# A sliding-window transformer kernel on one core: second norm and its loads moved ahead of the MLP weights, first three queries transposed by TensorE, work order found anew

## The chip, the cores and the metric

The kernel runs on one core of a Trainium2 chip. A core has five engines that run side by side, each through its own list of instructions in order: TensorE (PE, matrix products; PEld is its loading of weights), VectorE (DVE), ScalarE (ACT), GpSimd (POOL) and SyncE (SP), which here only issues DMAs. They wait for each other through semaphores. The metric is the device time of one execution in microseconds (us). Before the change the median of three runs is 863.51 us (863.23 to 866.3).

## The reference

Two layers, each of them attention followed by an MLP, on 2048 tokens of 576 numbers. Both layers use the same weights. Cut to what matters:

```python
D, H, Dh, W, F = 576, 32, 18, 256, 4608
def A(x):                                   # attention in a window of 256 keys
    q, k, v = split_heads(x @ wqkv)         # 32 heads of 18
    p = softmax(where(0 <= i - j < W, q @ k.T * Dh**-0.5, -1e9))
    return merge_heads(p @ v) @ wo
def B(x):                                   # MLP
    return gelu(layernorm(x) @ w1 + b1) @ w2 + b2
for _ in range(2):
    x = x + A(layernorm(x))
    x = x + B(layernorm(x))
```

`B` normalises its input, and it gets an input that is already normalised; the kernel makes both norms in one, by a changed scale.

## The kernel before, in words

The 2048 tokens are 16 tiles of 128. Four tiles make a chunk, so two layers make eight chunks, 0 to 7. For every chunk the kernel does these stages:

- `ln1_in` (layer 0) or `ln1` (layer 1): the norm. DVE takes statistics (`ln_stats`, L687 and L691), POOL makes 1/sqrt of the variance (`ln_rstd`, L700 and L702), DVE writes the normalised tile `xn` (L718), and `ln_norm_T` turns it (features onto partitions) into `xnTa`. For chunk 0 TensorE turns it (L735, copied from PSUM by ACT, L738), for all others a DMA transpose does (L741).
- `qkv`: projections to queries, keys and values. Chunk 0 uses whole-array matmuls (L797), chunk 1 matmuls that are packed by column groups or run over the whole array (`quad`, L781 and L778), later chunks row pairs (L837). DVE and ACT bring the results from PSUM into `qn` (L861, L858) or `vA` (L849, L847). Queries and keys are then turned into `qT` and `kT` by a DMA transpose on SP (L880), except the keys of chunk 0, which TensorE turns (L874) and ACT copies (L878). Chunk 1 keeps queries in a free half of `x_res` (`qx`) and two keys in `xnTm` (`kx`).
- `E0`/`E`: scores (L909), exponential on ACT (L919), the window mask on POOL (L940), product with the values (L957), division on DVE.
- `tail`: output projection (L1048), residual (L1025), second norm, turned into `xnTm[:, k % 2]` (resource `xm0_` or `xm1_`).
- `G_part`, `mm2`: the MLP in three thirds, first product L1093, GELU L1103, second product L778 or L781. Its weights come in slices from DRAM throughout (`w1_load`, `w2_load`).

Attention of one chunk and MLP of the chunk before it are issued in one mixed order. That order isn't written by hand. Every step is recorded with `add`, with a planned cost, a latency and a priority; `Plan.schedule` then places the steps one by one on the engine where one can start earliest by these costs, and breaks ties by priority. `PL.nudge` is a table of some 500 numbers that shift the priorities of named groups of steps, so it sets the order on all five engines. Until 140 us of its plan the planner also puts matmuls of zeros (`warm`, L674) where it foresees a wait of TensorE above 0.4 us.

The instructions of one engine run strictly in the order planned. A step whose input is late therefore holds up everything behind it on that engine, and that holds for SP's DMAs as well.

The start of the kernel, up to the first MLP matmul, is what the change touches by hand. There the loads stand on SP in this order: tiles 0 to 3 of x, the three weights of the projections, the first slice of `w1`, and only then tiles 4 to 7 of x, whose load names `xa3` (the last turned tile of chunk 0) as a resource it must follow:

```python
xin_load(4, 4, ["xa3"], -6)
...
xin_load(8, 4, ["k3"], -4)
...
ln1_in(1, -0.9)
```

Of the kernel before, what the change touches and what calls it, by code (L numbers as in the profile page):

```python
# [435 lines left out]
def build_kernel(nc, A_x, A_wqkv, A_wo, B_x, B_w1, B_b1, B_w2, B_b2, out):  # L436
    D = 576
# [13 lines left out]
    HB = 288  # L451
# [27 lines left out]
    PL.nudge = {"": -86.31, "b": 23.63, "ea0.0": -264.23, "ea0.1": 170.66, "ea0.2": 170.75, "ea0.p0": -91.12, "ea0.p1": 0.1, "ea0.p2":  # L479
# [150 lines left out]
    def xin_load(a, cnt, reads=(), prio=-10):  # L630
        dma("sp", x_in[:, a:a + cnt, :], x_dram[a * P:(a + cnt) * P, :].rearrange("(t p) d -> p t d", p=P), reads=reads,
            writes=[f"xin{t}" for t in range(a, a + cnt)], cls="x", ring=4,
            cost=0.6, prio=prio)
# [701 lines left out]
```

## Time and profile before

| what | us |
|---|---|
| median of three runs | 863.51 (863.23 to 866.3) |
| the profiled execution | 864.07 |
| its span, first to last instruction | 862.3 |
| TensorE busy in the span | 846.4 (98%) |
| ScalarE busy | 601.2 (70%) |
| VectorE busy | 395.7 (46%) |
| GpSimd busy | 378.6 (44%) |

The profile is one execution. Its page gives busy time by engine, the chain of work that ended last, and the costliest groups of instructions. Other views answer for a stretch of time: a timeline with one row for consecutive instructions of one line (start, duration, and in brackets the idle time before it with what ended it), a list of who waited for whom, and a table of stretches with the busy time of each engine and the granted TensorE clock. The span is 1.77 us shorter than the time of the same execution; that part lies outside what the trace shows.

### The profile page before, as it was taken

Reading aid. Unit: us, or ns where it says so; the run is one execution under the profiler, and the core shown is the slowest. Engines: PE = TensorE matmul, PEld = TensorE weight load, DVE = VectorE, ACT = ScalarE, POOL = GpSimd, SP = SyncE. Lnnn points to the kernel's source line nnn. Section 1 sums busy time; section 2 is a strip of 40 time slices with the busy share of each in tenths; the row PEclk is TensorE's granted clock in tenths of the full one; section 3 lists DMA queues with packets and bytes.
Section 4 is the critical chain, followed back from the end, with each engine's and each line's share of the span. In section 5 each row is a group of like instructions: output and inputs, shape, how many; then the busy total and the mean of one; then the engine's idle time right before and its main releaser. Section 6 shows DMA issues by size and latency. Waiting matters only on the chain.

```text
span 862.3 us, 27890 instructions
## 1 busy us (share of the span) xinstructions
PE 846.4 (98%) x12002; PEld 520.0 (60%) x12002; DVE 395.7 (46%) x949; ACT 601.2 (70%) x757; POOL 378.6 (44%) x563
## 2 busy tenths in 40 slices
PE   8899999999999999999999999999999999999998
PEld 6455556556565565666665655656556555556556
DVE  5787334644356442673426723465223633153012
ACT  5798797688757797476774878738777589853730
POOL 3787454375234662254522655416444276331100
PEclk9999999999999999999999999999999999999999
DMA  9798534743577524985359353594434963446320
GB/s 235 143 187 142 140 96 136 165 126 66 167 161 150 140 72 138 176 142 170 102 124 192 85 164 124 99 204 108 154 122 104 250 190 105 135 133 179 120 84 29
DMA packets 181995, 119.84 MB, mean 139 GB/s; under 512 B 107504, under 2 KB 181872, under 8 KB 181872
## 3 DMA queue, kind: packets, MB, share of 16 engines
q1 hardware_dynamic: 181872, 118.05, 55.6%
q8 instruction: 95, 1.56, 0.8%
q14 instruction: 28, 0.23, 0.1%
HBM read 90.10 MB, written 2.36 MB: 107 GB/s over the span
## 4 chain that ended last, share of the span: by engine, by line
PE 88%; DMA 4%; DVE 2%; POOL 2%; ACT 2%; issue 1%; SPq 0%; POOLq 0%; ACTq 0%
PE ps L1093 30%; PE ps L778 25%; PE ps L781 10%; PE ps L837 8%; PE ps L909 6%; PE ps L957 4%; PE ps L1048 3%; DMA xnTm<-xn 2%; ACT pT L919 1%; DMA xnTa<-xn 1%; PE ps L797 1%; POOL pT L940 1%; DVE xn L718 1%; DVE x_res L1025 1%; DMA qT<-qn 1%
## 5 line engine op out<-in xcount | busy, mean ns | idle before, releaser
L940 POOL TENSOR_SCALAR_AFFINE_SELECT pT<-pT 128x512 bf16<-128x512 bf16 (+1 forms) x368 | 284.3, 794 | 234.7 <-ACT pT L919 228.9
L919 ACT ACTIVATE pT<-ps 128x1024 bf16<-128x1024 f32 (+1 forms) x384 | 345.5, 972 | 49.9 <-PE ps L909 49.2
L1093 PE MATMUL ps<-xnTm,w_sb 64*128 64x512 bf16 x2592 | 290.9, 376 | 1.1 <-DVE vA L849 0.7
L1103 ACT ACTIVATE hT<-ps,b1col 128x512 bf16<-128x512 f32 x276 | 168.1, 688 | 175.3 <-PE ps L1093 175.0
L1093 PEld LDWEIGHTS ps<-xnTm,w_sb 64*128 64x128 bf16 x2592 | 129.6, 94 | 140.4 <-issue 4.8
L778 PE MATMUL ps<-w_sb,hT 128*128 128x288 bf16 x1446 | 193.7, 287 | 1.5 <-DVE x_res L1025 0.7
L1025 DVE TENSOR_TENSOR x_res<-ps,x_res 128x288 f32<-128x288 f32 x224 | 100.3, 453 | 183.5 <-PE ps L778 128.9
L778 PEld LDWEIGHTS ps<-w_sb,hT 128*128 128x128 bf16 x1446 | 133.6, 98 | 52.6 <-issue 17.1
L837 PE MATMUL ps<-wqkv,xnTa 64*128 64x288 bf16 x1296 | 90.8, 283 | 1.8 <-DMA xnTa<-xn 0.6
L781 PE MATMUL ps<-w_sb,hT 128*32 128x288 bf16 x2664 | 91.6, 286 | 0.2
L861 DVE CAST qn<-ps 128x288 bf16<-128x288 f32 x112 | 45.7, 448 | 99.1 <-PE ps L837 88.9
L837 PEld LDWEIGHTS ps<-wqkv,xnTa 64*128 64x128 bf16 x1296 | 61.6, 94 | 28.8 <-issue 3.1
L781 PEld LDWEIGHTS ps<-w_sb,hT 128*32 128x32 bf16 x2664 | 68.4, 97 | 14.9 <-issue 4.6
L968 DVE STREAM_TRANSPOSE oq<-ps 128x512 f32<-128x512 f32 x64 | 45.7, 714 | 66.6 <-PE ps L957 65.5
L909 PE MATMUL ps<-qT,kT 32*128 32x384 bf16 (+2 forms) x1216 | 64.2, 277 | 2.8 <-ACT pT L919 1.6
L700 POOL TENSOR_SCALAR vtmp<-mv_all 128x1 f32<-128x1 f32 (+1 forms) x43 | 8.9, 207 | 111.8 <-DVE mv_all L691 108.3
L687 DVE BATCH_NORM_STATS2 st_all<-x_res 128x6 f32<-128x288 f32 (+1 forms) x128 | 53.5, 445 | 9.0 <-DMA x_res<-in_A_x_dram 8.2
L1109 POOL TENSOR_TENSOR x_res<-x_res,b2bc 128x576 f32<-128x576 f32 x32 | 40.2, 1277 | 39.1 <-ACT hT L1103 38.9
L849 DVE CAST vA<-ps 128x288 bf16<-128x288 f32 x60 | 25.0, 447 | 56.6 <-PE ps L837 55.6
L957 PE MATMUL ps<-pT,vA 128*20 128x384 bf16 (+2 forms) x1408 | 50.4, 275 | 0.0
L909 PEld LDWEIGHTS ps<-qT,kT 32*128 32x128 bf16 x1216 | 19.4, 92 | 42.7 <-issue 29.8
L718 DVE TENSOR_SCALAR xn<-x_res,mv_all,rstd 128x576 bf16<-128x576 f32 (+1 forms) x60 | 34.4, 578 | 21.1 <-DMA xnTm<-xn 9.0
(58 smaller groups left out, 486.8 us busy)
## 6 DMA issues: line engine op xcount, KB each, us to landing
w_sb<-in_B_w_dram SPq DMA_DIRECT2D x46, 864.0 KB, 6.1
w_sb<-in_B_w_dram SPq DMA_DIRECT2D x48, 768.0 KB, 4.8
w_sb<-in_B_w_dram SPq DMA_DIRECT2D x96, 48.0 KB, 4.5
wqkv<-in_A_wqkv_dram SPq DMA_DIRECT2D x3, 576.0 KB, 4.8
x_res<-in_A_x_dram SPq DMA_DIRECT2D x3, 576.0 KB, 4.9
wqkv<-in_B_w_dram SPq DMA_DIRECT2D x2, 864.0 KB, 6.7
out_dram<-x_res SPq DMA_DIRECT2D x12, 144.0 KB, 1.8
wo_sb<-in_A_wo_dram SPq DMA_DIRECT2D x4, 144.0 KB, 3.0
```

The costliest lines, as they stand in the source:

```text
L687: add("dve", lambda e, i=i, s=s: e.bn_stats(st_all[:, t, i, :], s[:, t, i * HB:(i + 1) * HB]), reads=res, writes=[f"st{t}_{i}"], cost=0.37 ...
L778: return e.matmul(bank(b)[:, 0:HB], lhs, rhs, start=start, stop=stop, skip_group_check=True)
L781: ins = e.matmul(bank(b)[32 * j:32 * j + 32, 0:HB], lhs[:, 32 * j:32 * j + 32], rhs, start=start, stop=stop, tile_position=(0, 32 * j), sk ...
L837: ins = e.matmul(bank(bs[o])[:, 0:HB], xnTa[r:r + 64, c, i * 128:(i + 1) * 128], wqkv[r:r + 64, c, col:col + HB], start=(c == 4), stop=(ph ...
L861: add("dve", lambda e, b=bs[o], dst=dst: e.tensor_copy(dst, heads_of(bank(b))), reads=[bs[o]], writes=[f"qn{sl}h{o}"], cost=0.375, lat=0.1 ...
L909: ins = e.matmul(two(bs[j // 2])[:, j % 2, col:col + nq * 128], k_of(T0 + so)[0][32 * j:32 * j + 32, g, :], qs[32 * j:32 * j + 32, g, qo * ...
L919: add("act", lambda e, h2=h2: e.activation(pT[:, sl, 2 * h2:2 * h2 + 2, lo:hi], two(bs[h2])[:, :, lo:hi], ACT.Exp, scale=SCALE), reads=[bs ...
L940: add("pool", lambda e, ap=ap, pat=pat, sgn=sgn, kind=kind: e.affine_select(ap, ap, pattern=pat, compare_op=(ALU.is_ge if kind == "d" else ...
L957: ins = e.matmul(bank(bo)[32 * j:32 * j + VW, qo * 128:(qo + nq) * 128], vA[:, (T0 + so) % VS, 8 * j + g, :], pT[:, sl, j, col:col + nq * ...
L1025: add("dve", lambda e: e.tensor_tensor(x_res[:, t, sl], bank(b)[:, 0:HB], x_old[:, t, sl], ALU.add), reads=[b] + ([f"xin{t}"] if first els ...
L1093: ins = e.matmul(bank(bks[i])[:, 0:n], w1_sb[r:r + 64, sls[i], col:col + 128], xnTm[r:r + 64, k % 2, c, 0:n], start=(c == 4), stop=(ph == ...
L1103: add("act", lambda e, ff=ff, hd=hd, bk=bk: e.activation(hd[:, 0:n], bank(bk)[:, 0:n], ACT.Gelu_apprx_tanh, bias=b1col[:, ff:ff + 1]), rea ...
```

## The change

Seven edits, all in the planner's numbers or at the start of the kernel:

1. The load of tiles 4 to 7 of x no longer follows the turned tiles of chunk 0. It stands right behind the projection weights (priority -9.9).
2. The load of tiles 8 to 11 follows the last turned tile of chunk 1 instead of the last key of chunk 0.
3. Chunk 1's first norm writes into `xnTm[:, 0]` (`xm0_`), not into `xnTa`, so it needn't wait until chunk 0's projections have read `xnTa`. Its 1/sqrt is made for two tiles at a time, not four.
4. The first two slices of `w1` name `k3` (the last turned key of chunk 0) and `xm0_3` (the last turned norm tile of chunk 1) as what they follow. Before, one named `qx0`, which no step had written when the load was recorded, so it was free to go at once; the other named `v0h0`.
5. Queries 0, 1 and 2 of chunk 0 are turned by TensorE and copied by ACT, as the keys were already. Query 3 stays with a DMA transpose.
6. Planned costs of some loads and of the first zero matmuls differ, and a wait of the last partial transpose is stated more fully.
7. The nudge table is another one throughout, so the order differs on every engine from start to end.

```diff
-    PL.nudge = {"": -86.31, "b": 23.63, "ea0.0": -264.23, "ea0.1": 170.66, "ea0.2": 170.75, "ea0.p0": -91.12, "ea0.p1": 0.1, "ea0.p2":
...
+    PL.nudge = {"": -10.17, "b": -4.2, "ea0.0": 160.82, "ea0.1": 46.36, "ea0.2": -22.78, "ea0.p0": -231.95, "ea0.p1": 71.25, "ea1.0":
...
-            cost=0.6, prio=prio)
+            cost=0.45 if a < 4 else 0.6, lat=1.4 if a < 4 else 2.0, prio=prio)
...
-            writes=[f"w{w}A"], cost=0.6, prio=-10)
+            writes=[f"w{w}A"], cost=0.5, lat=1.9, prio=-10)
...
-        add("pe", lambda e, b=b: zero(e, b), reads=["warm"], writes=[b], cost=0.25, lat=0.2, prio=-7, alloc=[b])
+        add("pe", lambda e, b=b: zero(e, b), reads=["warm"], writes=[b], cost=0.42, lat=0.2, prio=-7, alloc=[b])
...
-                add("pe", fn, reads=rd[cs[0] // 4:][:1] + ["ident"], writes=[b], cost=0.1 * len(cs), prio=prio, alloc=[b] if cs[0] == 0 else ())
+                add("pe", fn, reads=rd[:1 + cs[0] // 4] + ["ident"], writes=[b], cost=0.1 * len(cs), prio=prio, alloc=[b] if cs[0] == 0 else ())
...
-            wr = [f"w{w}A", f"xa{i}"] + [f"w{w}{x}{b}" for x in "BC" for b in range(2)]
+            xT, xn_ = (xnTm[:, 0], "xm0_") if k == 1 else (xnTa, "xa")
+            wr = [f"w{w}A", f"{xn_}{i}"] + [f"w{w}{x}{b}" for x in "BC" for b in range(2)]
...
-                if k == 0 and (w == "k"):
+                if k == 0 and (w == "k" or w == "q" and i in (0, 1, 2)):
...
-    xin_load(4, 4, ["xa3"], -6)
+    xin_load(4, 4, ["wvA"] if False else [], -9.9)
...
-    xin_load(8, 4, ["k3"], -4)
...
-        ln_rstd(list(range(t0, t0 + nt)), False, prio)
+            if t % 2:
+                ln_rstd([t - 1, t], False, prio)
...
-            ln_norm_T(t0 + i, i, xnTa, "xa", prio, x_in, [f"xin{t0 + i}"], dup=True)
+            ln_norm_T(t0 + i, i, *((xnTm[:, 0], "xm0_") if k == 1 else (xnTa, "xa")), prio, x_in, [f"xin{t0 + i}"], dup=True)
...
+    xin_load(8, 4, ["xm0_3"], -0.8)
...
-                w1_load(-1, ["v0h0"])
+                w1_load(-0.7, ["xm0_3"])
...
-                w1_load(-1, ["qx0"])
+                w1_load(-1, ["k3"])
```

What stands on SP behind the projection weights, before the change. `w_sb` is a slice of MLP weights, `x_res` from `in_A_x_dram` a load of x, `hT` and `b2bc` the biases, `qT<-qn` a turned query tile, `xnTa<-xn` a turned norm tile:

```order
L626 DMA w_sb<-in_B_w_dram 128x4x768
L626 DMA w_sb<-in_B_w_dram 64x384 x2
L880 DMA_TRANSPOSE qT<-qn 128x8x128 x2
L626 DMA x_res<-in_A_x_dram 128x4x576
L880 DMA_TRANSPOSE qT<-qn 128x8x128
L626 DMA x_res<-in_A_x_dram 128x4x576
L626 DMA hT<-in_B_b_dram 36x128
L626 DMA b2bc<-in_B_b_dram 128x576
L880 DMA_TRANSPOSE qT<-qn 128x8x128
L626 DMA w_sb<-in_B_w_dram 128x4x768
L626 DMA w_sb<-in_B_w_dram 64x384 x2
L741 DMA_TRANSPOSE xnTa<-xn 128x5x128 x4
```

And after it:

```order
L625 DMA x_res<-in_A_x_dram 128x4x576
L740 DMA_TRANSPOSE xnTm<-xn 128x5x128 x3
L880 DMA_TRANSPOSE qT<-qn 128x8x128
L740 DMA_TRANSPOSE xnTm<-xn 128x5x128
L625 DMA x_res<-in_A_x_dram 128x4x576
L625 DMA hT<-in_B_b_dram 36x128
L625 DMA b2bc<-in_B_b_dram 128x576
L625 DMA w_sb<-in_B_w_dram 128x4x768
L625 DMA w_sb<-in_B_w_dram 64x384 x2
```

The load of x and the four norm transposes have moved ahead of both slices of `w1`, and three query transposes are gone from SP. Line numbers after the change are one lower in most of the file.

TensorE in the same stretch, from the first projections to the first score, before:

```order
L797 MATMUL ps<-wqkv,xnTa 128x288 x20
L735 MATMUL ps<-ident,xn 128x128 x10
L797 MATMUL ps<-wqkv,xnTa 128x288 x20
L874 MATMUL ps<-ident,qn 128x128 x8
L797 MATMUL ps<-wqkv,xnTa 128x288 x10
L874 MATMUL ps<-ident,qn 128x128 x8
L797 MATMUL ps<-wqkv,xnTa 128x288 x5
L874 MATMUL ps<-ident,qn 128x128 x8
L797 MATMUL ps<-wqkv,xnTa 128x288 x5
L909 MATMUL ps<-qT,kT 128x384 x4
```

And after, where the last row is again the first score:

```order
L734 MATMUL ps<-ident,xn 128x128 x6
L874 MATMUL ps<-ident,qn 128x128 x8
L796 MATMUL ps<-wqkv,xnTa 128x288 x10
L874 MATMUL ps<-ident,qn 128x128 x8
L796 MATMUL ps<-wqkv,xnTa 128x288 x5
L874 MATMUL ps<-ident,qn 128x128 x8
L796 MATMUL ps<-wqkv,xnTa 128x288 x15
L874 MATMUL ps<-ident,qn 128x128 x8
L734 MATMUL ps<-ident,xn 128x128 x4
L874 MATMUL ps<-ident,qn 128x128 x8
L734 MATMUL ps<-ident,xn 128x128
L909 MATMUL ps<-qT,kT 128x384 x4
```

Five groups of eight query and key transposes stand ahead of the first score instead of three, and 50 of the 120 projection matmuls of chunk 0 instead of 70; two more such groups follow later instead of one.

DVE, before, from the second fetched query or key on. `BN_STATS` and `BN_AGGR` are the statistics, here those of chunk 1, and `CAST` is a result fetched from PSUM:

```order
L861 CAST qn<-ps 128x2x8x18
L718 TENSOR_SCALAR xn<-x_res,mv_all,rstd 128x576
L861 CAST qn<-ps 128x2x8x18 x4
L687 BN_STATS st_all<-x_res 128x6 x3
L691 BN_AGGR mv_all<-st_all 128x2
L687 BN_STATS st_all<-x_res 128x6 x2
L691 BN_AGGR mv_all<-st_all 128x2
```

And after:

```order
L717 TENSOR_SCALAR xn<-x_res,mv_all,rstd 128x576
L861 CAST qn<-ps 128x2x8x18
L686 BN_STATS st_all<-x_res 128x6 x3
L690 BN_AGGR mv_all<-st_all 128x2
L686 BN_STATS st_all<-x_res 128x6
L861 CAST qn<-ps 128x2x8x18
L690 BN_AGGR mv_all<-st_all 128x2
L686 BN_STATS st_all<-x_res 128x6 x3
L861 CAST qn<-ps 128x2x8x18
```

The first statistics of chunk 1 stood behind six fetched query and key results; now they stand behind three, and the fourth and fifth are fetched between them.

More of the change, by code (lines that the diff above doesn't have):

```diff
@@ L823, in qkv @@
             dest = [f"v{A % VS}h{o}" for o in range(2)] if w == "v" else [f"qn{qn_ctr[0] % NQN}h{o}" for o in range(2)]
-            wr = [f"w{w}A", f"xa{i}"] + [f"w{w}{x}{b}" for x in "BC" for b in range(2)]
+            xT, xn_ = (xnTm[:, 0], "xm0_") if k == 1 else (xnTa, "xa")
+            wr = [f"w{w}A", f"{xn_}{i}"] + [f"w{w}{x}{b}" for x in "BC" for b in range(2)]
             if k < KF:
-                bs = two_out(lambda c: xnTa[:, c, i * 128:(i + 1) * 128], lambda c, s, n=n: wqkv[:, c, n * D + s:n * D + s + HB],
+                bs = two_out(lambda c: xT[:, c, i * 128:(i + 1) * 128], lambda c, s, n=n: wqkv[:, c, n * D + s:n * D + s + HB],
                              wr, prio + 0.01 * n, after=dest, fill=(6, 7) if k == 1 else FILL, mode="c" if k == 1 else "f")
```

127 rows, old and new, of the table add are left out of this document.

## Prediction

> **What bounds the kernel now.** I read the page first, then the list of who waited for TensorE's inputs, then the table of stretches, and last the timelines of the first 60 us. The page says that TensorE is busy almost throughout:
>
> ```profile
> PE 846.4 (98%) x12002; PEld 520.0 (60%) x12002; DVE 395.7 (46%) x949; ACT 601.2 (70%) x757; POOL 378.6 (44%) x563
> ```
>
> The stretches show where the missing 2% lie. The columns are the stretch, its length, busy time (and instructions) of PE, PEld, DVE, ACT and POOL, granted clock, DMA share and GB/s:
>
> ```profile
> 6.00:20.40 14.40, 12.64 (x124) 9.87 (x123) 7.62 (x21) 8.86 (x17) 2.98 (x7) 1.00 1.03 252
> 20.40:29.40 9.00, 8.74 (x83) 5.46 (x81) 8.44 (x29) 8.08 (x12) 6.25 (x12) 1.00 0.93 225
> 29.40:34.00 4.60, 2.00 (x50) 1.18 (x50) 2.58 (x8) 1.95 (x4) 3.15 (x6) 0.99 0.84 86
> 34.00:38.00 4.00, 4.00 (x27) 1.94 (x25) 1.76 (x6) 3.01 (x4) 2.98 (x5) 0.58 0.47 92
> 38.00:60.00 22.00, 20.36 (x335) 11.95 (x327) 19.01 (x42) 20.23 (x28) 16.48 (x24) 1.00 0.91 153
> 60.00:75.00 15.00, 14.62 (x262) 9.02 (x263) 10.61 (x25) 13.78 (x21) 10.47 (x16) 1.00 1.08 219
> 75.00:89.60 14.60, 12.99 (x203) 7.07 (x198) 10.35 (x29) 13.51 (x20) 11.44 (x26) 1.00 0.70 94
> 90.00:700.00 610.00, 606.97 (x9091) 372.89 (x9090) 286.46 (x681) 438.96 (x538) 279.06 (x403) 1.00 0.57 139
> ```
>
> From 90 to 700 us TensorE is idle for 3.0 us of 610. A new order can win little there and can only lose. Before 90 us there are three kinds of loss: waits, a stretch at 0.58 of the clock, and from 38 us on an ACT that is busy for 47.5 of 51.6 us (92%) and nearly a second bound. The long waits, and the pace before and after them, stand in TensorE's timeline (start, duration, line, operation, idle before it in brackets):
>
> ```profile
> 9.33 2.61 PE L797 MATMUL ps<-wqkv,xnTa 128*128 128x288 bf16 x20
> 11.78 0.72 PE L735 MATMUL ps<-ident,xn 128*128 128x128 bf16 x10
> ...
> 14.87 0.61 PE L874 MATMUL ps<-ident,qn 128*128 128x128 bf16 x8
> 15.32 1.39 PE L797 MATMUL ps<-wqkv,xnTa 128*128 128x288 bf16 x10
> ...
> 20.06 0.34 PE L909 MATMUL ps<-qT,kT 32*128 32x384 bf16 x4 [1.23 <-DMA qT<-qn]
> ...
> 32.37 0.80 PE L781 MATMUL ps<-wqkv,xnTa 128*32 128x288 bf16 x20 [2.60 <-DMA xnTa<-xn]
> ...
> 33.87 1.36 PE L778 MATMUL ps<-wqkv,xnTa 128*128 128x288 bf16 x5
> 35.16 0.51 PE L909 MATMUL ps<-qT,kT 32*128 32x384 bf16 x4
> 35.59 2.23 PE L778 MATMUL ps<-wqkv,xnTa 128*128 128x288 bf16 x10
> ...
> 39.53 0.79 PE L778 MATMUL ps<-wqkv,xnTa 128*128 128x288 bf16 x5
> ...
> 43.60 1.40 PE L778 MATMUL ps<-wqkv,xnTa 128*128 128x288 bf16 x10
> ```
>
> **Why chunk 1's norm is late.** SP's timeline shows its queue. The load of tiles 4 to 7 goes out at 13.73, behind MLP weights and two query transposes; the four norm transposes go out from 26.85, right behind another slice of MLP weights:
>
> ```profile
> 7.59 1.78 SPq L626 DMA_DIRECT2D w_sb<-in_B_w_dram  x3
> 9.56 4.12 SPq L880 DMA_TRANSPOSE qT<-qn  x2
> 13.73 0.59 SPq L626 DMA_DIRECT2D x_res<-in_A_x_dram  x1
> ...
> 24.52 1.57 SPq L626 DMA_DIRECT2D w_sb<-in_B_w_dram  x3
> 26.85 7.06 SPq L741 DMA_TRANSPOSE xnTa<-xn  x4
> ```
>
> The chain of waits has the first of these four as its longest piece between 20 and 40 us, 5.48 us, while the four together (the view of that tile) landed within 2.6 to 5.5 us. So the first landed slowest, and it is the one behind the weights:
>
> ```profile
> 26.85 5.48 DMA xnTa<-xn
> ```
>
> ```profile
> DMA to landing us min/median/max: 2.6/3.6/5.5
> ```
>
> **The change, part by part.** *Second norm.* The load of tiles 4 to 7 takes the place on SP that the weights had, at 7.59. Its landing is bounded by the load that stood there and by loads of its own size, which the DMA view of the first 40 us gives:
>
> ```profile
> w_sb<-in_B_w_dram SPq DMA_DIRECT2D x2, 768.0 KB, 5.7
> x_res<-in_A_x_dram SPq DMA_DIRECT2D x2, 576.0 KB, 4.5
> ```
>
> So it lands between 12.1 and 13.3, where it landed near 19:
>
> ```profile
> 19.00 1.18 DVE L687 BATCH_NORM_STATS2 st_all<-x_res 128x6 f32<-128x288 bf16 x3 [2.41 <-DMA x_res<-in_A_x_dram]
> ```
>
> The norm then runs some 6 us earlier, its transposes have no weights ahead of them, and the tiles lie ready by about 25 us, when TensorE needs them near 30. The 2.60 us wait goes. The slow stretch after it should go with it: against the rows at full clock it cost (1.36 - 0.79) + (2.23 - 1.40) + (0.51 - 0.34) = 1.57 us. A 2.60 us wait was followed by it here, a wait of 1.23 us by none.
>
> [...]
>
> *Queries by TensorE.* Three DMA transposes leave SP, and with them the 1.23 us wait. TensorE gets 24 more transposes. Eight of them took 15.32 - 14.87 = 0.45 us from start to start, so 1.35 us, all of it on the engine that sets the end. ACT gets three copies like that of a key:
>
> ```profile
> 15.52 1.01 ACT L878 COPY kT<-ps 128x1024 bf16<-128x1024 bf16 x1
> ```
>
> Until 20.4 ACT is idle for 5.5 us of 14.4, which hides most of it. If that cover is gone, 3 x 1.01 us come into the path of the first exponentials. The first score now needs five groups of turned tiles: TensorE's work ahead of it (40 projection matmuls of (11.78 - 9.33)/20 = 0.12, five groups of eight transposes of 0.45, 11 norm transposes at an eighth of that, from 9.33) ends at 17.1, and ACT's copies can push it to 18.4. Before, it stood at 20.06; but 20 projection matmuls now come after it, so this is no gain beyond the wait that I have counted.
>
> *New waits.* Query 3 keeps its DMA, now behind three norm transposes on SP: issued near 21, it lands after 3.0 to 5.1 us by the row of L880 up to 34 us, while the fourth score wants it near 24.6. That is 0 to 1.5 us.
>
> ```profile
> DMA to landing us min/median/max: 3.0/4.9/5.1
> ```
>
> In chunk 1 the third query tile in line (`qx2`) is issued six TensorE steps ahead of that chunk's first score, where the last one stood twelve ahead before. The steps between are worth 1.40 + 1.40 + 3 x 0.34 + 0.66 = 4.5 us, against a fetch of 0.46 and a landing of 3.0 to 5.1: 0 to 1.1 us. The fetch on DVE and the value product on TensorE are these rows:
>
> ```profile
> 33.22 0.46 DVE L861 CAST qn<-ps 128x288 bf16<-128x288 f32 x1 [1.99 <-PE ps L781]
> ```
>
> ```profile
> 38.66 0.66 PE L957 MATMUL ps<-pT,vA 128*20 128x384 bf16 x16
> ```
>
> Together with the first that is 0 to 2.6 us; I take 1.0, nearer the fast landings, since the weights no longer run beside them.
>
> *Moved without cost.* The `w1` slices go out some 15 us later and are first read near 89. The load of tiles 8 to 11 moves from 19.3 to about 24 and feeds a norm that TensorE needs near 62. One more pair of 1/sqrt on POOL falls where POOL is busy for 2.98 of 14.4 us. Fewer zero matmuls at the start (22 instead of 27 ahead of the first projection) let the first norm transposes start up to 0.5 us sooner, but the projection also waits for its weights; I take 0.2. The planned costs that differ do nothing by themselves.
>
> *The new order from 90 us on.* TensorE's work is the same: the same number of first and second MLP products, scores and projections. 54 of the column-packed groups of four (L781) become whole-array matmuls (L778), by the page's groups
>
> ```profile
> L778 PE MATMUL ps<-w_sb,hT 128*128 128x288 bf16 x1446 | 193.7, 287 | 1.5 <-DVE x_res L1025 0.7 <-DVE vA L849 0.7
> ...
> L781 PE MATMUL ps<-w_sb,hT 128*32 128x288 bf16 x2664 | 91.6, 286 | 0.2
> ```
>
> 193.7/1446 = 0.134 against 4 x 91.6/2664 = 0.138 us, so -0.2 us at most, and I count nothing. Changes of the array's tiling number 408 before and 411 after. Whether the 3.0 us of waits there grow can't be read from the order; I take 0, with -1 to +3.
>
> The sum: -2.60 - 1.57 - 1.23 + 1.35 - 0.2 + 1.0 = -3.25 us. The profiled execution took 864.07, so 860.8; it is 0.56 us above the median of the runs, and against the median it is 860.3 us. A gain before 90 us reaches the end, since TensorE has no idle time behind it that could swallow it.
>
> **The rivals.** *More is won.* No new wait appears, and the later waits of the start, which come from fetches and scores that are late, go too:
>
> ```profile
> PE ps L778 <- DVE vA L849: 1.6, 2, 1.0
> PE ps L909 <- ACT pT L919: 1.6, 6, 0.4
> ...
> PE ps L1093 <- DVE vA L849: 0.7, 1, 0.7
> ```
>
> That is another 1.0 and at most 3.9 us; with 2.4 of them 860.3 - 1.0 - 2.4 = 856.9. For it speaks that chunk 1's norm casts leave the crowded stretch from 25 to 31 us; against it that ACT is 92% busy.
>
> *ACT takes the gain.* Behind its first exponential ACT now has two fetches (0.46 each by the row of DVE) and one key copy (1.01) more than before, 1.9 us. If ACT sets the pace there, 860.3 + 1.9 = 862.2. Against it: ACT waited for TensorE for 2.65 us in the stretch from 29.4 and for about 1 us in the next.
>
> *Slower: DVE is blocked by early statistics.* Chunk 1's statistics now stand on DVE ahead of the fetches of the fourth query or key. If the load lands not at 13 but at 19 as before, the fetch ends at 19.0 + 1.18 + 0.39 (one more statistic) + 0.46 = 21.0, and with a turn (0.45) and a copy (1.01) the first score comes at 22.5, 4.5 us later than the 18 I expect, with another slow stretch of 1.57 us: 866.4. Each us that the load lands after about 14 costs one; slower than before from about 17 on. The packed DMA queue (share 1.03 up to 20.4) speaks for it, the place directly behind the weights against.
>
> *The clock drops over transposes.* Up to the first score nearly half of TensorE's time from 11 us on is now transposes. The rows show transposes at the full clock, but three groups only. If such a stretch let the clock fall once, as after 34 us, the price is 1.57: 861.9.
> [...]
>
> *The new order has its own late places.* With a new wait of 0.5 us at each of seven chunks, 3.5 us, the gain is gone: 863.8.
>
> **How the numbers follow.** The forecast case has a chance of 0.40 (859 to 862 by itself), more won 0.23, ACT 0.12, the clock 0.05, the new order 0.10, the blocked DVE 0.10. What a measurement can tell from no change is about 0.5%, 4.3 us: below 859.2 is faster, above 867.8 slower. Faster gets the second case and about a third of the first, 0.36; slower gets half of the blocked DVE and half of the new order, whose waits can be longer than 0.5 us, 0.10; the rest, 0.54, is within 0.5%. The range reaches from 856.5, most of the second case, to 866.5, the blocked DVE.
>
> **What would show it.** No wait of TensorE for a turned norm tile near 30 us and a clock of 1.00 in all stretches up to 90 show the first two terms right. The first score before 19 us shows the queries right. The first MLP matmul (L1093), at 89.62 before, should start near 86.4; if it does and the end doesn't follow, the new order has lost it later. Statistics of chunk 1 that begin after 15 us, or a slow clock before 20, would make the prediction wrong.

## The result

| | before | after |
|---|---|---|
| median, us | 865.23 (862.9 to 868.64) | 861.77 (860.46 to 864.78) |
| profiled execution, us | 864.07 | 861.1 |
| its span, us | 862.3 | 859.4 |

The ratio is 0.9963, with an interval of 0.9951 to 0.9976: 3.2 us faster (2.1 to 4.2), which is within the 0.5% that the forecast counted as no change. The kernel before, measured again beside it, has a median 1.7 us above the one that the forecast started from, so the forecast of 860.3 (3.2 us less than 863.51) has the difference right and the level 1.5 us too low.

The page of the kernel after, engines over the whole span:

```profile
PE 845.8 (98%) x11851; PEld 516.0 (60%) x11851; DVE 398.0 (46%) x949; ACT 602.3 (70%) x760; POOL 380.6 (44%) x567
```

Its stretches (length, busy time of PE, PEld, DVE, ACT, POOL, granted clock, DMA share, GB/s):

```profile
6.00:20.40 14.40, 11.98 (x115) 9.09 (x114) 8.90 (x29) 8.49 (x16) 4.90 (x12) 0.88 0.45 146
20.40:29.40 9.00, 8.85 (x88) 5.89 (x86) 3.58 (x9) 9.00 (x15) 4.60 (x10) 1.00 0.63 110
29.40:34.00 4.60, 4.57 (x77) 2.95 (x69) 3.22 (x9) 3.25 (x5) 3.56 (x5) 1.00 0.91 254
34.00:38.00 4.00, 3.92 (x68) 2.41 (x64) 3.99 (x14) 3.94 (x6) 2.05 (x3) 1.00 1.20 336
38.00:60.00 22.00, 19.99 (x321) 11.52 (x314) 18.35 (x46) 21.71 (x31) 20.40 (x32) 1.00 0.96 162
60.00:75.00 15.00, 13.68 (x230) 8.01 (x230) 11.71 (x27) 12.07 (x17) 8.44 (x13) 1.00 1.20 218
90.00:700.00 610.00, 608.66 (x8962) 370.14 (x8960) 291.83 (x686) 440.92 (x541) 281.66 (x404) 1.00 0.56 139
```

From 29.4 to 38 us the hole and the clock of 0.58 are gone. A clock of 0.88 has appeared before 20.4, ACT has no idle time from 20.4 to 29.4, and from 38 to 75 us TensorE idles for 3.3 us where it idled for 2.0. From 90 us on it idles for 1.34 us where it idled for 3.03. TensorE's timeline and SP's, at the places of the forecast:

```profile
8.48 2.56 PE L796 MATMUL ps<-wqkv,xnTa 128*128 128x288 bf16 x10 [2.05 <-DMA wqkv<-in_A_wqkv_dram]
...
19.95 0.34 PE L909 MATMUL ps<-qT,kT 32*128 32x384 bf16 x4 [0.30 <-ACT qT L878]
...
32.45 0.80 PE L780 MATMUL ps<-wqkv,xnTm 128*32 128x288 bf16 x20
...
88.40 3.85 PE L1093 MATMUL ps<-xnTm,w_sb 64*128 64x512 bf16 x34
```

```profile
8.48 0.59 SPq L625 DMA_DIRECT2D x_res<-in_A_x_dram  x1
19.95 3.95 SPq L740 DMA_TRANSPOSE xnTm<-xn  x3
23.99 1.26 SPq L880 DMA_TRANSPOSE qT<-qn  x1
25.30 1.28 SPq L740 DMA_TRANSPOSE xnTm<-xn  x1
```

Chunk 1's first projection (32.45) no longer waits, and the first score waits 0.30 us for ACT, not 1.23 for a DMA. But the first score is not at 18: TensorE could start on the query weights only at 8.48, and the ten projections behind that wait ran at half pace (2.56 us, where ten take 1.39 at full clock). And the first MLP product starts at 88.40, only 1.22 us earlier than before, not 3.25.

### The profile page after: what moved, and what is told of

Read it like the earlier page. It is cut to its first block, busy times and chain, and to the rows that moved or that the text cites. A ratio compares the mean times of both kernels' runs of the same rounds, so it can differ in the third digit from the quotient of the medians.

```text
span 859.4 us, 27561 instructions
## 1 busy us (share of the span) xinstructions
PE 845.8 (98%) x11851; PEld 516.0 (60%) x11851; DVE 398.0 (46%) x949; ACT 602.3 (70%) x760; POOL 380.6 (44%) x567
## 4 chain that ended last, share of the span: by engine, by line
PE 90%; DMA 3%; ACT 2%; DVE 2%; issue 1%; POOL 0%; SPq 0%; POOLq 0%; ACTq 0%; DVEq 0%
PE ps L1093 32%; PE ps L777 25%; PE ps L780 9%; PE ps L837 8%; PE ps L909 6%; PE ps L957 4%; PE ps L1048 4%; ACT pT L919 2%; PE ps L796 2%; DMA xnTm<-xn 1%; DMA kT<-qn 1%; DMA wqkv<-in_A_wqkv_dram 1%; DVE oq L968 0%; DVE x_res L1025 0%; DMA qT<-qn 0%
## 5 line engine op out<-in xcount | busy, mean ns | idle before, releaser
L1093 PEld LDWEIGHTS ps<-xnTm,w_sb 64*128 64x128 bf16 x2592 | 127.6, 94 | 142.3 <-issue 4.5
L777 PE MATMUL ps<-w_sb,hT 128*128 128x288 bf16 x1500 | 201.1, 287 | 0.4 <-DVE x_res L1025 0.4
L777 PEld LDWEIGHTS ps<-w_sb,hT 128*128 128x128 bf16 x1500 | 138.5, 98 | 53.4 <-issue 16.4
L780 PE MATMUL ps<-w_sb,hT 128*32 128x288 bf16 x2448 | 84.8, 286 | 0.1
L780 PEld LDWEIGHTS ps<-w_sb,hT 128*32 128x32 bf16 x2448 | 63.4, 97 | 12.8 <-issue 3.7
L699 POOL TENSOR_SCALAR vtmp<-mv_all 128x1 f32<-128x1 f32 (+2 forms) x45 | 9.2, 204 | 119.1 <-DVE mv_all L690 117.6
L1048 PE MATMUL ps<-wo_sb,attT 64*128 64x288 bf16 x576 | 42.7, 283 | 0.4
```

Of the source, the lines that this page charges most:

```text
L777: return e.matmul(bank(b)[:, 0:HB], lhs, rhs, start=start, stop=stop, skip_group_check=True)
L780: ins = e.matmul(bank(b)[32 * j:32 * j + 32, 0:HB], lhs[:, 32 * j:32 * j + 32], rhs, start=start, stop=stop, tile_position=(0, 32 * j), sk ...
L1048: ins = e.matmul(bank(bs[o])[:, 0:HB], attT[r:r + 64, c, i * 128:(i + 1) * 128], wo_sb[r:r + 64, c, col:col + HB], start=(ph == 0 and c == ...
L1093: ins = e.matmul(bank(bks[i])[:, 0:n], w1_sb[r:r + 64, sls[i], col:col + 128], xnTm[r:r + 64, k % 2, c, 0:n], start=(c == 4), stop=(ph == ...
```

## The experiments

All ratios are to the kernel before, measured on the same chip at the same time. "The changed kernel" is the kernel after. Where an edit moves a step, the order of everything else stays as it was: the move is made on the finished plan.

**Both kernels again.** Unaltered, to see what one profile is worth.

> The changed kernel once more, unaltered. In its first profile the weights of the queries landed at 8.35 us (7.09 in the profile before the change), TensorE waited 2.05 us for them at 8.48, and ten projections behind that wait ran at about half pace. Theory 'chance of one execution': here they land near 7.1, the granted clock of 6 to 20.4 us is 1.00 again, the first score starts near 18 instead of 19.95 and the first MLP product near 86.5 instead of 88.40. Theory 'of the kernel': the wait is 2 us again and the milestones stay where they were (19.95, 88.40). Either way the time against the kernel before is again about -3.4 us.

> The kernel before the change once more, unaltered, one profile. In the profile that the prediction read, the query weights were there at 7.6 us; in three of the four later profiles they came at 7.8 to 8.5. Theory 'that profile was a favourable execution': here the first projection after the zero matmuls starts at 8 us or later, the wait for a turned query is about 2 us instead of 1.23, and the first MLP product starts at 90.5 to 91.5 instead of 89.62. Rival: it repeats 7.6, 1.23 and 89.62 within 0.3. In both cases the time from the first MLP product to the end is 769.5 us, as in the two profiles with the old order (769.53 and 769.48).

The changed kernel again has a ratio of 0.9961 (0.9945 to 0.9976). TensorE's rows of it, and behind them those of the kernel before, with its stretch from 90 us:

```profile
8.31 1.39 PE L796 MATMUL ps<-wqkv,xnTa 128*128 128x288 bf16 x10 [1.43 <-DMA wqkv<-in_A_wqkv_dram]
...
18.95 0.34 PE L909 MATMUL ps<-qT,kT 32*128 32x384 bf16 x4 [0.31 <-ACT qT L878]
...
88.70 3.63 PE L1093 MATMUL ps<-xnTm,w_sb 64*128 64x512 bf16 x32
```

```profile
21.84 0.34 PE L909 MATMUL ps<-qT,kT 32*128 32x384 bf16 x4 [2.18 <-DMA qT<-qn]
...
34.01 1.39 PE L781 MATMUL ps<-wqkv,xnTa 128*32 128x288 bf16 x20 [2.46 <-DMA xnTa<-xn]
...
91.52 0.82 PE L1093 MATMUL ps<-xnTm,w_sb 64*128 64x512 bf16 x6 [1.05 <-DMA xnTm<-xn]
```

```profile
90.00:700.00 610.00, 606.29 (x9061) 372.15 (x9058) 285.78 (x681) 439.02 (x539) 278.26 (x403) 1.00 0.57 139
```

Neither theory on the changed kernel is quite right: the weights were late again (8.31), but the half pace did not come, and although the first score came 1 us earlier, the first MLP product came 0.3 us later. Of the kernel before, the profile that the forecast read was a good execution: here the wait for turned queries is 2.18 us, not 1.23, and the first MLP product 1.9 us later. Means of two profiles each: the first MLP product starts at 90.57 before and 88.55 after, so 2.0 us are won ahead of it; the spans are 863.05 and 860.0, so 1.0 us is won behind it. The milestone is a fair one: but for zero matmuls and the 24 query transposes, the same number of matmuls of each kind stands ahead of it in both orders.

All profiles in one table. "Behind it" is the span less the start of the first MLP product; "slow" is the stretch in which the granted clock was 0.50, read in slices of 0.2 us from 5 to 69 us.

| kernel | first score | first MLP product | behind it | slow |
|---|---|---|---|---|
| before | 20.06 | 89.62 | 772.7 | 33.8 to 37.4 |
| b_again | 21.84 | 91.52 | 772.3 | 34.0 to 37.6 |
| b_w1_behind | 21.83 | 91.40 | 772.6 | 21.8 to 25.2 |
| after | 19.95 | 88.40 | 771.0 | 8.0 to 11.6 |
| a_again | 18.95 | 88.70 | 771.9 | none |
| a_q_dma | 19.40 | 89.64 | 771.1 | 20.4 to 24.0 |
| a_dve_copies | 19.45 | 90.78 | 770.3 | 7.8 to 11.4 |
| a_w1_first | 20.57 | 89.05 | 770.9 | 8.2 to 11.8 |
| a_w1_both | 20.58 | 90.47 | 770.4 | 19.2 to 22.8 |
| a_warm | 17.53 | 88.82 | 771.5 | none |
| a_wo_late | 17.65 | 89.60 | 770.5 | none |
| a_warm_wo | 17.95 | 88.39 | 770.8 | none |
| a_wo_early | 19.43 | 89.73 | 771.8 | 8.0 to 11.6 |
| a_warm_wo_early | 18.73 | 88.50 | 770.5 | none |

With the new order the part behind lasts 770.3 to 771.9 us in every profile, with the old 772.3 to 772.7. The means differ by 1.55 us. TensorE is busy for 766.1 us of it in both profiles of the kernel before, and for 765.9 and 766.1 in both of the changed kernel; so it is idle time that shrinks, from 6.4 to 5.5 us on average in these four. a_w1_both and a_q_dma, described below, undo two of the hand-made edits and keep the short part (770.4 and 771.1), so it goes with the rest of the change, above all the order. No run has the new order with the whole of the old start.

**The second w1 slice alone, in the kernel before.**

```diff
 SP order:
-    w1 slice (3 DMAs), then xnTa<-xn x4
+    xnTa<-xn x4, then w1 slice (3 DMAs)
```

> The kernel before the change, with one move: the second slice of w1 (three DMAs) stands on SP behind the four norm transposes of chunk 1 instead of ahead of them. Order of all else as before. Theory of the prediction: the first transpose lands in about 3 us instead of 5.5, the wait of 2.60 us at 32.37 shrinks to 0.5 or less and the stretch of 34 to 38 us runs at a granted clock of 1.00 instead of 0.58: the first MLP product starts 3 to 4 us earlier (near 86 instead of 89.62), and the end follows by the same 3 to 4 us. Rival 'other cause': the tile is late through its fetch, 1/sqrt or the query transposes: the wait stays above 2 us, time within 1 us of before. Rival 'the clock has its own rhythm': the wait goes, the slow stretch stays: 2 to 2.6 us won. Rival 'something else bounds chunk 1' (ACT, 92% busy): the wait goes, but less than 1.5 us is left of it at the first MLP product.

Ratio 0.9997 (0.9985 to 1.0009): no gain, and by the interval 1.3 us at most. TensorE's, SP's and DVE's rows (line numbers are five higher than before in this kernel):

```profile
21.83 0.51 PE L914 MATMUL ps<-qT,kT 32*128 32x384 bf16 x4 [2.18 <-DMA qT<-qn]
...
33.05 0.80 PE L786 MATMUL ps<-wqkv,xnTa 128*32 128x288 bf16 x20
...
45.46 0.79 PE L783 MATMUL ps<-wqkv,xnTa 128*128 128x288 bf16 x5 [0.88 <-DVE qn L866]
```

```profile
30.20 7.05 SPq L746 DMA_TRANSPOSE xnTa<-xn  x4
37.31 1.78 SPq L631 DMA_DIRECT2D w_sb<-in_B_w_dram  x3
39.27 1.50 SPq L885 DMA_TRANSPOSE x_res<-qn  x1
```

```profile
44.95 0.46 DVE L866 CAST qn<-ps 128x288 bf16<-128x288 f32 x1 [1.44 <-DMA x_res<-qn]
```

This profile and b_again have their first score within 0.01 us of each other, so they compare well. The wait for turned norm tiles is gone, as the forecast's mechanism says, and so is the slow stretch behind it. But a slow stretch came at 21.8 instead, behind a wait that had no such effect in b_again (the last section sets the two side by side). Chunk 1's first projections are therefore only 0.96 us ahead of b_again (33.05 against 34.01). By 38 us, once b_again is through its own slow stretch, the lead is 1.44. The rest is lost at the queries of chunk 1: the slice that no longer stands ahead of the norm transposes stands directly ahead of the first query transpose, DVE waits 1.44 us until that transpose has read `qn`, and TensorE 0.88 us for DVE. At the first MLP product 0.12 us is left. So the first transpose was late behind the weights, but the wait moved on to the next item of SP's list. The timed runs agree: 7 of these 12 had a mean clock of 1.000, so no slow stretch, against 5 of 32 of the kernel before beside them, yet those seven took 865.15 us on average and those five 863.63.

**The loads' places, undone in the changed kernel.** First the one slice, then both.

```diff
 SP order of a_w1_first:
-    x tiles 4-7, ..., w1 slice, w1 slice
+    w1 slice, x tiles 4-7, ..., w1 slice
 SP order of a_w1_both:
-    x tiles 4-7, xnTm<-xn x3, ..., w1 slice, w1 slice
+    w1 slice, x tiles 4-7, w1 slice, xnTm<-xn x3, ...
```

> The changed kernel with the first slice of w1 ahead of the load of x tiles 4 to 7 on SP, as before the change; order of all else as in the changed kernel. The load then lands about 2.8 us later, near 16.7 instead of 13.88. Theory of the prediction's rival 'DVE is blocked by early statistics': the fetches of queries and keys behind the statistics are late by about as much; the first score starts 1.5 to 3 us later and the end is 1.5 to 3 us later, up to 4.5 with a slow stretch. Rival 'DVE has room': the first score waits for ACT anyway, within 0.5 us of the changed kernel.

> As the changed kernel with the first slice of w1 ahead of the load of x tiles 4 to 7, and the second slice too moved ahead, to directly before the first norm transpose of chunk 1 (the places that they had before the change); order of all else as in the changed kernel. Theory 'the loads' places are the gain': the first turned norm tile takes 5 us or more to land instead of 3, TensorE waits for it or for query 3 by 1 us or more, and the end is 1.5 us or more behind that of the kernel with the first slice alone moved. Theory 'slack': turned norm tiles are needed only near 32 us, so the second slice costs less than 0.5 us beyond the first.

Ratios 0.9972 (0.9961 to 0.9983) and 0.9985 (0.9971 to 1.0): against 0.9963 that is 0.8 us and 1.9 us given back. The intervals overlap with the changed kernel's, the first one by much, so the sizes are rough; by mean times, 863.0 and 864.5 against 862.0 in 25 runs of the changed kernel, they are 1.0 and 2.5 us. DVE's first statistics of chunk 1 in a_w1_first, TensorE's late rows there, and the same two rows in a_w1_both:

```profile
16.21 1.18 DVE L693 BATCH_NORM_STATS2 st_all<-x_res 128x6 f32<-128x288 bf16 x3 [1.69 <-DMA x_res<-in_A_x_dram]
```

```profile
18.23 0.79 PE L803 MATMUL ps<-wqkv,xnTa 128*128 128x288 bf16 x5 [0.87 <-DVE qn L868]
...
28.67 0.34 PE L916 MATMUL ps<-qT,kT 32*128 32x384 bf16 x4 [0.70 <-DMA qT<-qn]
```

```profile
17.99 0.79 PE L807 MATMUL ps<-wqkv,xnTa 128*128 128x288 bf16 x5 [2.02 <-DVE qn L872]
...
30.14 0.34 PE L920 MATMUL ps<-qT,kT 32*128 32x384 bf16 x4 [1.30 <-DMA qT<-qn]
```

The forecast's blocked DVE is real: with statistics at 16.21, and not at 14.85 as in the profile after, TensorE waits 0.87 us for a fetch behind them (2.02 in a_w1_both). The price is nearer 1 than the 1.5 to 3 us expected. The second slice costs 1.1 us more, between the two theories. The wait that grew with it is the one for query 3, which stands behind the norm transposes on SP (1.30 us against 0.70); none is for a norm tile.

**Queries by DMA again.**

```diff
-    queries 0, 1, 2: 8 TensorE transposes and an ACT copy each
+    queries 0, 1, 2: one DMA transpose on SP each
```

> The changed kernel, with queries 0, 1 and 2 turned by DMA transposes on SP again; order of all else as in the changed kernel. TensorE loses 24 transposes (1.35 us), ACT three copies (3 us), SP gets three DMAs. Theory 'TensorE's turning is worth it' (the prediction's terms): the first score waits for a turned query by 1 us or more, and the time is 0 to +1.5 us against the changed kernel. Rival 'ACT bounds the ramp': ACT, 9.00 of 9.00 us busy from 20.4 to 29.4, starts its exponentials earlier, and the first MLP product and the end come 1 to 2 us sooner.

Ratio 0.9975 (0.9959 to 0.9991), 1.0 us given back, which by the overlapping intervals isn't clear of noise; but the wait is there:

```profile
19.40 0.34 PE L924 MATMUL ps<-qT,kT 32*128 32x384 bf16 x4 [1.84 <-DMA qT<-qn]
...
89.64 2.55 PE L1108 MATMUL ps<-xnTm,w_sb 64*128 64x512 bf16 x22 [0.46 <-ACT pT L934]
```

ACT had 6.71 us of work instead of 9.00 from 20.4 to 29.4, and this won nothing. The first theory fits.

**ACT relieved.**

```diff
-    query 3, keys 2 and 3 of chunk 0: 3 fetches and 2 copies on ACT
+    the same on DVE
```

> The changed kernel, with the late fetches and key copies of chunk 0 (query 3, keys 2 and 3: three fetches of about 0.5 us, two copies of about 1 us) on DVE instead of ACT; order of all else as in the changed kernel. DVE is busy for 3.58 of 9.00 us from 20.4 to 29.4, ACT for 9.00. Theory 'ACT bounds the ramp': TensorE's waits for exponentials shrink and the first MLP product starts 1.5 to 3 us earlier, with the end 1.5 to 3 us earlier (about 859 if the changed kernel has 861.5). Rival 'ACT is full but not the bound': less than 0.7 us. Rival 'DVE becomes late': its fetches wait behind statistics and value casts, and the end comes 1 us or more later.

Ratio 0.9962 (0.9949 to 0.9976), as the changed kernel. The stretch, and TensorE's later rows:

```profile
20.40:29.40 9.00, 8.90 (x90) 6.12 (x89) 6.24 (x14) 6.93 (x10) 4.85 (x9) 1.00 0.65 115
```

```profile
50.87 0.79 PE L788 MATMUL ps<-wqkv,xnTm 128*128 128x288 bf16 x5 [1.09 <-DVE qn L872]
...
53.35 0.79 PE L788 MATMUL ps<-wqkv,xnTm 128*128 128x288 bf16 x5 [1.42 <-DVE oq L979]
```

ACT's load falls to 6.93, and the time does not move. ACT is full there, but is not by itself the bound: waits for DVE near 51 us are longer instead (one of 0.36 us in the profile after, 0.53 and 0.83 in a_again).

**No wait for the weights.**

```diff
-    3 zero matmuls ahead of the first projections
+    12 zero matmuls
```

> The changed kernel with nine more zero matmuls of 0.14 us (1.2 us in all) on TensorE right ahead of the first projections, where it waits 1.4 to 2.1 us for the query weights; order of all else as in the changed kernel. Theory 'idle time brings a slow stretch': in two of four profiles with the new order 3.3 us at a granted clock of 0.50 followed this wait; with it filled, the clock is 1.00 up to 20 us, and the median is 0.3 to 1.0 us below the changed kernel (861.7). Rival 'hidden': what is lost there lies beside the waits for ACT that follow, and the time stays within 0.3. Rival 'too many': the matmuls last longer than the wait, 0.3 us or more slower.

Ratio 0.9958 (0.9942 to 0.9973). The granted clock is 1.00 from 5 to 88 us, and the first score the earliest of all. But the zero matmuls are not shown to have done it: the query weights came early here, with the first projection at 7.35, and a_wo_late below, which has no more zero matmuls than the changed kernel, starts it at 7.33, has the same clock and its first score at 17.65. Rows of TensorE, DVE and SP:

```profile
17.53 0.34 PE L911 MATMUL ps<-qT,kT 32*128 32x384 bf16 x4 [0.31 <-ACT qT L880]
...
51.47 0.79 PE L779 MATMUL ps<-wqkv,xnTm 128*128 128x288 bf16 x5 [1.62 <-DVE oq L970]
```

```profile
48.28 0.46 DVE L863 CAST qn<-ps 128x288 bf16<-128x288 f32 x1 [1.65 <-DMA x_res<-qn]
```

```profile
38.38 5.00 SPq L627 DMA_DIRECT2D wo_sb<-in_A_wo_dram  x9
43.43 1.24 SPq L882 DMA_TRANSPOSE x_res<-qn  x1
```

The rival "hidden" is nearest: 2.4 us at the first score are 0.4 us to the wrong side at the first MLP product. DVE waits for a query transpose that SP issued late, after 5 us of issuing `wo_sb`.

**Ten wo_sb DMAs behind those transposes**, without and with the zero matmuls. The expectations count nine; one more stands ahead of the group of nine, and the edit moves it too.

```diff
 SP order:
-    x_res<-qn, wo_sb, xnTm<-qn, wo_sb x9, x_res<-qn, xnTm<-qn
+    x_res<-qn, xnTm<-qn, x_res<-qn, xnTm<-qn, wo_sb x10
```

> The changed kernel with nine DMAs of the output projection's weights (wo_sb), which SP issues for 5.4 us from 36.7 to 44.9, moved behind the query and key transposes of chunk 1 that stood behind them (44.92 and 46.26); they are first read at 70.84. Order of all else as in the changed kernel. Theory 'the query transposes behind wo_sb hold chunk 1': the transposes go out 2 to 3 us earlier, DVE's fetch that waits for one of them (0.56 us, 1.65 with the warm matmuls) no longer waits, TensorE's waits for oq and for exponentials from 50 to 61 us shrink, and the end comes 0.5 to 1.5 us earlier than the changed kernel (861.7). Rival 'ACT is full there': ACT's exponentials run without a break from 37.6 to 56.8 in the changed kernel, so nothing is won without an earlier start: within 0.3 us.

> Both moves: nine more zero matmuls ahead of the first projections, and the nine wo_sb DMAs behind the query and key transposes of chunk 1. With the zero matmuls alone the first score started at 17.53 instead of 19.95 or 18.95 and nothing of it was left at the first MLP product (88.82 against 88.40 and 88.70): TensorE idled for 2.5 us of 7 from 45 to 52, where a DVE fetch waited 1.65 us for a query transpose. Theory 'that transpose, late behind wo_sb, swallowed it': the idle time there falls below 1.2 us, the first MLP product starts near 87, and the time is 1.2 to 2.2 us below the changed kernel, about 860. Rival 'the next engine swallows it': the wait moves to ACT or to the key transpose at 67 us, and the time is within 0.5 us of 861.7.

Ratios 0.9983 (0.997 to 0.9997) and 0.9968 (0.9954 to 0.9982): no gain on the changed kernel. The first is 1.7 us behind it, the second 0.4 us, which is within the noise. TensorE and SP of a_wo_late:

```profile
61.63 0.34 PE L914 MATMUL ps<-x_res,xnTm 32*128 32x384 bf16 x4 [2.67 <-issue]
```

```profile
41.33 1.37 SPq L885 DMA_TRANSPOSE x_res<-qn  x1
...
44.50 5.80 SPq L630 DMA_DIRECT2D wo_sb<-in_A_wo_dram  x10
...
58.23 1.30 SPq L885 DMA_TRANSPOSE x_res<-qn  x1
```

The transposes that stood behind `wo_sb` go out from 41.33, 3.6 us earlier than in the changed kernel (44.92) and 2.1 us earlier than in a_warm (43.43), whose first score is as early. The waits for DVE near 50 us are gone, and the first chunk-1 score with a later query waits 2.67 us at 61.63. Its query was issued at 58.23. The profile names no releaser for this wait; that it is the query is read from the score starting 3.37 to 3.41 us after that issue in all eleven profiles of the changed order, among them a_warm_wo (57.19 and 60.59) and the changed kernel (57.42 and 60.81); in the three with the old order it starts 5.2 to 6.5 us after it. Again the wait moved on.

**All twelve wo_sb DMAs early**, where SP is idle, without and with the zero matmuls.

```diff
 SP order:
-    x tiles 4-7, xnTm<-xn x3, ..., wo_sb x12 among the query transposes
+    x tiles 4-7, wo_sb x12, xnTm<-xn x3, ...
```

> The changed kernel with all twelve DMAs of wo_sb directly behind the load of x tiles 4 to 7, where SP stands idle from 9.1 to 19.95 us; order of all else as in the changed kernel. Moved behind the query transposes instead (the run before), they took the wait with them: TensorE's idle time went from 45 to 52 us to a 1.8 to 2.7 us wait at 60 us, for a query whose transpose SP issued at 57 to 58, and the time rose by 1.5 to 2 us. Theory 'SP's list bounds chunk 1': with 6.5 us of issues gone from 35 to 52 us, that query goes out 1 to 3 us earlier, the waits from 45 to 61 us shrink and the end comes 1 to 2 us earlier than the changed kernel (861.7). Rival 'ACT bounds it': no gain above 0.3 us. Rival 'the loads collide': the twelve DMAs delay the landing of x tiles 4 to 7 (13.88) and the first score: 1 us or more slower.

> The same with nine more zero matmuls ahead of the first projections. Theory 'SP's list bounds chunk 1': the first score near 17.5 now pays: the first MLP product starts at 86 to 87.5 instead of 88.4 to 88.8, and the median is 1.5 to 3 us below the changed kernel, near 859.5. Rival 'ACT bounds it': first MLP product at 88 or later, median within 0.5 us of 861.7.

Ratios 0.9957 (0.9939 to 0.9974) and 0.9941 (0.992 to 0.9962), medians 862.24 and 860.99. TensorE's rows of the second:

```profile
18.73 0.34 PE L917 MATMUL ps<-qT,kT 32*128 32x384 bf16 x4 [0.15 <-ACT qT L886]
...
60.23 0.34 PE L917 MATMUL ps<-x_res,xnTm 32*128 32x384 bf16 x4 [0.39 <-ACT pT L927]
...
66.91 0.40 PE L917 MATMUL ps<-x_res,kT 32*128 32x256 bf16 x8 [0.99 <-DMA kT<-qn]
...
88.50 3.85 PE L1101 MATMUL ps<-xnTm,w_sb 64*128 64x512 bf16 x34 [0.40 <-ACT pT L927]
```

DVE's waits for late transposes between 45 and 61 us (1.65 us at 48.28 in a_warm) are gone; what is left of TensorE's are waits of 0.2 to 0.4 us for ACT and DVE and one for a key's DMA near 67. One of them still hangs on the late query, though its row names ACT: the score at 60.23 starts 3.40 us after the issue at 56.83. The first MLP product does not come earlier for it (88.50), so with `wo_sb` out of the way SP's list alone does not bound chunk 1. The rival "the loads collide" has a part in that: the load of x tiles 4 to 7 lands 6.9 and 6.8 us after its issue in the two, where it took 5.4 and 5.0 in the changed kernel's profiles, and with the zero matmuls the first score comes 1.2 us later than in a_warm. The combined kernel has the lowest median of all, 0.7 us below the changed kernel's (1.9 us by the ratios); but the two intervals overlap, so that it beats the changed kernel isn't shown. What sets 88.4 as a floor stays open. Every edit that relieved ACT or SP ended in a wait for another engine, as it would if all their lists were nearly as late as TensorE's; no run relieves them all at once.

## Why the prediction was right, and where it was not

The total was right: 3.25 us forecast, 3.2 measured by the ratio. The split was not, and that the two totals agree so closely is luck: 2.0 us were won ahead of the first MLP product and not 3.25, and about 1.0 us behind it and not 0.

- **The 2.60 us wait and the slow stretch behind it (4.17 us).** Both are gone as forecast, by the mechanism named. But 4.17 us was the size of two gaps, not what they are worth: in the old order their removal brought no gain (0.9997), in the new order the loads' places are worth about 1.9 us. The failed step is "A gain before 90 us reaches the end, since TensorE has no idle time behind it that could swallow it". Between 38 and 90 us there was little idle TensorE time before the change, but an earlier start was turned into waits for SP, DVE and ACT: from 38 to 75 us TensorE idled for 2.0 us before, 3.3 and 4.5 in the two profiles after, and 5.7 in a_warm, which had the earliest first score.
- **Queries by TensorE (1.23 won, 1.35 paid).** The wait is 1.84 us when the DMA transposes come back, and 2.18 in the second profile of the kernel before; 1.23 was a good execution. The whole part is worth about 1.0 us net, where the forecast made it slightly negative.
- **New waits (+1.0).** In the changed kernel's two profiles query 3 and `qx2` cost nothing. In a_wo_late query 3 cost 0.69 us, in a_warm_wo_early 0.78, within the 0 to 1.5 given for it.
- **First score near 18.** 19.95 and 18.95, because the query weights let TensorE start at 8.48 and 8.31 us, not at 7.64 as in the profile read, and because a slow stretch cost another 1.2 us in the first of the two. In a_wo_late, which is the changed kernel up to 36 us, the start was 7.33 and the first score at 17.65, inside the 17.1 to 18.4 worked out.
- **First MLP product at 86.4.** It came at 88.40 and 88.70. Against the mean of two profiles before, 2.0 us of the 3.25 were won there.
- **The new order from 90 us on (0).** This is the step that made up for it: TensorE idles there for 1.34 and 2.00 us in the two profiles after, 3.03 and 3.71 before, 1.7 us less up to 700 us. To the end 0.9 us of that is left, and the part behind the first MLP product is 1.0 to 1.55 us shorter. "Can win little there and can only lose" contradicts itself: 3 us of idle time was something to win. The gain lies at or beyond the edge of the range of -1 to +3.
- **The rivals.** A blocked DVE needs a late load, and the load was early (13.88 us, and statistics at 14.85 instead of 19.00). Transposes did not lower the clock: in a_again the stretch up to 20.4 has five groups of them and a clock of 1.00. ACT is as full as that rival feared, but moving its copies away won nothing.
- **The signs.** No wait for a norm tile near 30 us, and statistics of chunk 1 at 14.85: these came as forecast. A first score before 19 came in one of two profiles (18.95), the first MLP product near 86.4 in none. The slow clock before 20, named as a sign of being wrong, came in the profile after (0.88) and not in a_again. It stood behind the wait for the query weights, for which the forecast's sum has no loss; the last section shows how little it cost.

## What to carry over

A wait with a slow stretch behind it was an upper bound on a gain here, not its size: 4.17 us were counted, and in the old order their removal brought none (0.9997). Before adding such a wait up, look at how late the other engines' lists, and the DMA-issuing engine's above all, run in the stretch behind it. Moving a load on a full issuing list handed the wait to the next step (1.44 us of DVE in b_w1_behind, 2.67 us of TensorE in a_wo_late); only moving it into the list's idle time took DVE's waits away here, and even that did not move the first MLP product (88.50 in a_warm_wo_early). And one profile is one draw: the landing of the query weights set the start anywhere from 7.33 to 8.48 us with the changed order, so where a landing does that, take two or three profiles before a term is sized from it.

## What the runs showed of the hardware

The slow stretches are all alike: every one has the clock at 0.50 for 3.41 us (read in slices of 0.2 us, 3.40 to 3.42), which is 1.7 us of lost work. In the 3.41 us ahead of each, TensorE was busy for 0.96 to 1.57 us. A wait of 1.40 us in a_wo_early had one with it:

```profile
7.80 2.34 PE L802 MATMUL ps<-wqkv,xnTa 128*128 128x288 bf16 x10 [1.40 <-ACT xn L728]
```

A wait of 2.18 us in b_again was followed by none, and the same wait at the same time in b_w1_behind by one. So here the length of the wait alone doesn't tell.

The trace's record of the granted clock has the same length again. In the profile before, it is 27.31 us at full clock (6.62 to 33.93), 3.41 at 0.50 and then 826.03 at full, which are 8, 1 and 242 times 3.413; in the profile after, it starts with 3.41 at full (4.77 to 8.18) and 3.41 at 0.50. So each of the nine profiles with a slow stretch can be cut, from the edges of that stretch, into pieces of 3.41 us. The wait of 2.18 us in b_again is shared by two pieces, 16.98 to 20.40 and 20.40 to 23.81, in which TensorE is busy for 2.68 and 1.97 us; in b_w1_behind it lies in one, 18.38 to 21.79, with 1.27 us, and the slow stretch follows. Of the pieces that start at 4.4 us or later and end by 69 us, the one ahead of the slow stretch has the least work in each of the nine (0.96 to 1.57 us); the next in all of them has at least 1.65 us (b_w1_behind, from 4.73). Laid otherwise, 3.41 us don't show it: in the profile before, those from 28.98 hold only 0.81 us of work, and the clock falls at 33.93, not at their end. In the profiles without a slow stretch the edges can't be read. In a_again no 3.41 us from 5 to 69 us, laid in steps of 0.2 us, hold less than 1.61 us of work (7.00 to 10.41), but in a_warm, a_wo_late and a_warm_wo there are some with 1.07, 0.74 and 1.42 us (from 48.0, 58.4 and 57.2), and the clock stays at 1.00. Measured is the agreement in these nine profiles; what sets the clock is not shown.

The mean granted clock of each timed execution is read here as a count of its slow stretches. That is an estimate: one is 1.7 of 862 us, 0.002 of the clock, and in the profiled executions a mean of 0.998 goes with one slow stretch (nine profiles), 1.000 with none (four), and a_warm has 0.999 with none from 5 to 88 us. Mean times by it, over 17, 51 and 21 executions before and 11, 6, 3 and 4 after:

| mean clock | 1.000 | 0.998 | 0.996 | 0.994 to 0.995 |
|---|---|---|---|---|
| before, us | 863.93 | 865.62 | 867.23 | none |
| after, us | 861.39 | 861.62 | 862.66 | 864.00 |

Before, each costs 1.6 to 1.7 us; after the change the first costs 0.2 us, as far as six executions can tell. In the profiles of the changed order four of six fall between 8 and 12 us, where the table of profiles shows no gain from an earlier first score. So 2.5 us of the difference are there with no slow stretch at all, and the rest, about 1 us, goes with slow stretches that cost less, since there are about as many (one per execution on average) before and after.
